# Left rows and left probabilities in idle slots of the left tile, and 576 columns of one weight granule kept in SBUF

## The chip, the cores and the metric

One core of one Trainium2 chip runs the kernel. The metric is the device time of one execution in microseconds; lower is better. In the profile the engines are PE (matrix products), PEld (its weight loads), DVE (VectorE), ACT (ScalarE), POOL (GpSimd) and SP (SyncE); 16 transfer engines move data between HBM and SBUF.

## The reference

```python
xn = layernorm(x)                         # x: 2048 rows of 1024
mem = mem0                                # 8 rows
for s in range(64):                       # segments of 32 rows, in order
    h = concat(mem, xn[32*s : 32*s+32])   # 40 rows
    q, k, v = h @ Wq, h @ Wk, h @ Wv      # 32 heads of 128
    p = softmax(mask(q @ k.T * 128**-0.5))
    o = (p @ v) @ Wo
    mem = o[:8]; out[32*s : 32*s+32] = o[8:]
result = x + out + B(xn)                  # B: two rows picked by a router go through a gated MLP, the others pass
```

Every segment needs the memory rows that the segment before has made, so the 64 segments run one after the other, and each uses all four weight matrices: 32 MB in bf16, more than SBUF holds.

## The kernel before, in words

The weights are cut into 64 granules of 128 partitions x 2048 columns (512 KB). Granules 0 to 47 are the six phases of a segment (query, key, query, key, value, value halves, eight granules each), granules 48 to 63 the sixteen steps w of the output projection. 44 granules are resident in SBUF (tiles `wres`). The other twenty are streamed in every segment through five slots (pool `wstream`, tile `g`): `fetch` (L329) issues the load on SP's queue from a packed copy in DRAM (`wsc`), and `after` calls it as soon as the granule that held a slot has been used. Granule 11 is kept whole in PSUM (`KEPT`), so its slot is filled by four copies and no load; of granule 25, columns 1024 to 2047 are kept in PSUM and copied into the slot (L349), columns 0 to 1023 are loaded: 256 KB, from a `wsc` copy of that width.

The order of the work is written out by hand: every engine carries out its instructions in the order in which the program emits them. `hook(p, kc, fn)` puts `fn` behind granule kc of phase p; `todo` is a list of such entries for the next segment; inside the projection the code names w.

A segment's main pass treats 24 of its 32 rows and the 8 memory rows (`ST`, L645). The remaining 8 rows of four segments in a row, s = 4G to 4G + 3, form one "left" tile of 32 rows that goes through the weights once for the four (`STL`, `left_pass` at L628): its queries are made in segment j = 1, its keys in j = 2, its values in j = 0 of its own group (j = s mod 4). Queries and keys go by DRAM (`ql_d`, `LX`) to each segment. The attention of each segment treats main and left rows together: `scores`, `exponent`, `soften` (L552 to L563) and `attend` (products L578 and L580, copies L585 and L587). The left outputs of segment j are written to slot j of `OTL` (128 x 4 x 8 x 32), and in j = 3 `project(WL, ...)` (L700) multiplies the four slots by the output weights, the last five steps of it as `todo` in the next segment.

Tiles that the change touches:

- `PL` (128 x 256): the probabilities that belong to the left keys, eight columns per block for segment j, zeros elsewhere. POOL clears the columns of the segment before at (1, 0) (L591), `soften` writes them (L560) and transposes the tile (L563).
- `XL` (128 x 256): the left rows of x, loaded by four DMAs on POOL's queue (L289), once in j = 0 for the next group's normalization (`norm_left`, L294) and once in j = 3 for the sum (`sum_left`, L303; added to `WL` by an identity product, L738, at w = 1).
- the scratch for the left queries, slots 2 and 3 of `OTL`: ACT copies PSl there and issues the store to `ql_d` (L669, L672).
- `OTL` itself, made at its first use in a group.

Of the kernel before, what the change touches and what calls it, by code (L numbers as in the profile page):

```python
# [20 lines left out]
KEPT_PART = 25  # L21
LEFT_OUT = 35
NEG = -30000.0

# [4 lines left out]
def kernel(  # L29
# [17 lines left out]
    P = 128  # L47
# [46 lines left out]
    const = ctx.enter_context(tc.tile_pool(name="const", bufs=1))  # L94
    dram = ctx.enter_context(tc.tile_pool(name="dram", bufs=1, space=DRAM))
    wstream = ctx.enter_context(tc.tile_pool(name="wstream", bufs=N_SLOT))
    one = ctx.enter_context(tc.tile_pool(name="one", bufs=1, reuse_waits="tile"))
    psA = ctx.enter_context(tc.tile_pool(name="psA", bufs=2, space=PSUM))
    psL = ctx.enter_context(tc.tile_pool(name="psL", bufs=1, space=PSUM))
# [8 lines left out]
    def columns(g, s):  # L108
        if s > 0 and g == KEPT_WHOLE:
            return None  # L110
        return slice(0, 1024 if s > 0 and g == KEPT_PART else 2048)

# [13 lines left out]


    IDENT = const.tile([P, P], BF16, name="IDENT")
    make_identity(nc, IDENT[:, :])

    XS = const.tile([P, 256], BF16, name="XS")
    XN = const.tile([P, 256], BF16, name="XN")
    PL = const.tile([P, 4, 2, 32], BF16, name="PL")
    CT = const.tile([P, 32], F32, name="CT")
# [14 lines left out]
    nc.vector.memset(XN[:, :], 0.0)  # L149
    nc.gpsimd.memset(PL[:, :, :, :], 0.0)  # L150
    nc.vector.memset(NMSK, 0.0)
# [123 lines left out]
    def new_st(s):  # L275
        PTx = turn(XN)
        st = one.tile([P, KC, SEG], BF16, tag="st", name="ST")
        nc.scalar.copy(out=gview(st)[:, :, :, 0:XM], in_=PTx[:, :, :, 0:XM])
        return st
# [4 lines left out]

    def load_left(G):
        t = one.tile([P, 256], BF16, tag="xl", name="XL")
        o4 = x2[4 * G * SEG:4 * (G + 1) * SEG, :].rearrange("(s r) d -> s r d", s=4)
        for g in range(4):
            nc.gpsimd.dma_start(out=t[32 * g:32 * (g + 1), :], in_=o4[:, XM:SEG, 256 * g:256 * (g + 1)])  # L289
        return t  # L290
# [40 lines left out]

    def part(t, jq):
        return t[:, 512 * jq:512 * (jq + 1)]


    def keep(g, t):
        for c, K in KEPT_COLS[g].items():
            turned = PTB.rearrange("p (i r) -> p i r", i=4)
            for i in range(4):
                nc.tensor.transpose(out=turned[:, i, :], in_=t[:, 512 * c + P * i:512 * c + P * (i + 1)],  # L340
                                    identity=IDENT[:, :])
            XK = one.tile([P, 512], BF16, tag="vl", name="XK")
# [47 lines left out]
    load_seg(0)  # L390
    XL0 = load_left(0)
    OB = one.tile([P, 256], BF16, tag="bA", name="MEM0")
# [102 lines left out]
    for s in range(NSEG):  # L495
# [53 lines left out]
        def soften(half):  # L549
            S8 = SPS.rearrange("p i a k -> p (i a) k")  # L550
            DN = one.tile([P, 8], F32, tag="nm", name="DN")
            nc.vector.tensor_reduce(out=DN[:, :], in_=S8, axis=AX.X, op=ALU.add)  # L552
            nc.vector.reciprocal(out=DN[:, :], in_=DN[:, :])
            PT2 = one.tile([P, 2, 4, 64], BF16, tag=("bA", "bE")[half], name="PT2")
            PTm, PTl = PT2[:, 0], PT2[:, 1]
            PM = PTl.rearrange("p i q -> p (i q)").rearrange("p (b k) -> p b k", b=8)
            PLt = PL.rearrange("p i a k -> p (i a) k")
            dnb = DN[:, :].unsqueeze(2)
            nc.vector.tensor_tensor(out=PM, in0=S8[:, :, 0:32], in1=dnb.to_broadcast([P, 8, 32]), op=ALU.mult)
            nc.vector.tensor_tensor(out=PLt[:, :, XL * j:XL * (j + 1)], in0=S8[:, :, 32:NK],  # L560
                                    in1=dnb.to_broadcast([P, 8, XL]), op=ALU.mult)
            nc.vector.transpose(out=PTm.rearrange("p i q -> p (i q)"), in_=PM.rearrange("p b k -> p (b k)"))
            nc.vector.transpose(out=PTl.rearrange("p i q -> p (i q)"), in_=PLt.rearrange("p b k -> p (b k)"))  # L563
            PTs[half] = (PTm, PTl)

        def attend(half, ph):
# [15 lines left out]
            for jl in range(2):  # L582
# [4 lines left out]
                copy(out=left_out()[:, j, :, h0:h0 + 4].rearrange("p r i -> p i r"), in_=ov[:, :, SEG:NK])  # L587

        def clear_pl():
            jp = (j + 3) % 4  # L590
            nc.gpsimd.memset(PL.rearrange("p i a k -> p (i a) k")[:, :, XL * jp:XL * (jp + 1)], 0.0)  # L591

        def get_left():
            nxt["xl"] = load_left(G if j == 3 else G + 1)

        def prep_left():
            if j == 0:
                norm_left(nxt["xl"], G + 1)
            else:
                sum_left(nxt["xl"], G)  # L600

        for at, fn in todo:
            hook(*at, fn)
        todo = []
        hook(1, 0, clear_pl)
        if s > 0:
# [8 lines left out]
        if s + 1 < NSEG:  # L615
            hook(2, 0, lambda: load_seg(s + 1))
        if j == 3 or (j == 0 and G + 1 < NT):
            hook(2 if j else 3, 0, get_left)
            hook(5, 3, prep_left)
# [5 lines left out]

        def left_pass(PSl, g, Gv, first_, last_):
            for jq in range(4):
                nc.tensor.matmul(PSl[32 * jq:32 * jq + 32, :], lhsT=STL[:, g % KC, :], rhs=part(Gv, jq),  # L628
                                 start=first_, stop=last_, tile_position=(0, 32 * jq))

        left_before = False
        for p, (mat, half) in enumerate(PHASES):
# [8 lines left out]
            for kc in range(KC):  # L641
                g = 8 * p + kc
                Gv = granule(g)
                for jq in range(4):
                    nc.tensor.matmul(PSm[32 * jq:32 * jq + 32, :], lhsT=ST[:, kc, :], rhs=part(Gv, jq),  # L645
                                     start=(kc == 0), stop=(kc == KC - 1), tile_position=(0, 32 * jq))
# [12 lines left out]
            if mat < 2:  # L659
# [35 lines left out]

        def project(PS, w, Gv, lhs, last):
            for hs in range(2):
                h = 2 * w + hs
                for g in range(4):
                    nc.tensor.matmul(PS[32 * g:32 * g + 32, 0:256], lhsT=lhs(h),  # L700
                                     rhs=Gv[:, D * hs + 256 * g:D * hs + 256 * (g + 1)], start=False,
                                     stop=(last and hs == 1), tile_position=(0, 32 * g), skip_group_check=True)
# [12 lines left out]
        late = home_w[len(carried):]  # L715
        final = (carried or late or [None])[-1]
        behind = []
        for w in range(16):
# [8 lines left out]
            if j == 3:  # L727
                if w in home_w:
                    fn = lambda w=w, Gv=Gv: project(WL, w, Gv, lhs_left, w == final)
                    if w in late:  # L730
# [5 lines left out]
                if w == 1:  # L736
                    WL = psL.tile([P, 512], F32, tag="accl", name="WL")
                    nc.tensor.matmul(WL[:, 0:256], lhsT=IDENT[:, :], rhs=nxt["xl"][:, :], start=True, stop=False,  # L738
                                     skip_group_check=True)
                if w >= 1:  # L740
                    for w_, Gv_ in behind:
                        project(WL, w_, Gv_, lhs_left, False)
# [26 lines left out]
        for fn in fill[n1:]:  # L769
            fn()  # L770
        if j == 3:
            def store_left(G=G, WL=WL):
                OL = one.tile([P, 256], BF16, tag="vl", name="OL")
                nc.scalar.copy(out=OL[:, :], in_=WL[:, 0:256])
                o4 = out2[4 * G * SEG:4 * (G + 1) * SEG, :].rearrange("(s r) d -> s r d", s=4)
                for g in range(4):
                    nc.gpsimd.dma_start(out=o4[:, XM:SEG, 256 * g:256 * (g + 1)], in_=OL[32 * g:32 * (g + 1), :])
            todo.append(((2, 4), store_left))
        if s + 1 < NSEG:
# [118 lines left out]
```

## Time and profile before

| | |
|---|---|
| median of 3 runs | 1993.74 us (1986.56 to 2001.2) |
| the profiled execution's own time | 1984.53 us |
| its span, first to last instruction | 1982.9 us, mean granted clock 0.957 |
| PE busy | 1630.3 us (82%) |
| DVE, ACT, POOL busy | 883.9, 733.5, 436.4 us |
| moved by DMA | 712.42 MB, mean 359 GB/s |

The span is one profiled execution; the three runs scatter around a time some 9 us longer. The program has three parts: the first segment with the loading of the resident weights, 63 segments of about 28 us, and the gated MLP at the end. Groups of instructions are named by line, engine, and written tile<-read tiles; behind the bar stand busy time, mean of one, and the idle time of the engine before them with what ended it. A row of the timeline has start, duration, engine, line and operation.

### The profile page before, as it was taken

The numbers are of one execution on the slowest core, as the hardware profiler recorded it, in microseconds if no ns is written. First come the engines' busy times: TensorE is split into PE (matmuls) and PEld (weight loads), VectorE is DVE, ScalarE is ACT, GpSimd is POOL, SyncE is SP. The second block draws the span as 40 slices with busy tenths as digits, with TensorE's granted clock in tenths as the row PEclk, the third lists the DMA queues.
The fourth block names the chain that finished last, engine by engine and source line by source line (L and its number), as shares of the span: only waits on it lengthen the run. The fifth ranks groups of instructions, "written<-read, shape, count | busy, mean of one in ns | idle before, by whom it ended". The sixth has DMA issues, their size and how long they took to land. (4 is left out here: it accounts for less than half of the span.)

```text
span 1982.9 us, 82788 instructions
## 1 busy us (share of the span) xinstructions
PE 1630.3 (82%) x36080; PEld 893.2 (45%) x36080; DVE 883.9 (45%) x2848; ACT 733.5 (37%) x1995; POOL 436.4 (22%) x883
## 2 busy tenths in 40 slices
PE   3468898989888888989888888989888898988863
PEld 1224444444454444445454444545444444544443
DVE  5834444444444434444454444444444444444430
ACT  1124343434334343433444344443434343343330
POOL 3112213112221311222121221222131122212110
PEclk8669999999999999999999999999999999999995
DMA  9999999999999999999999999999999999999998
GB/s 370 403 340 371 353 358 347 366 362 348 375 336 367 366 336 357 360 367 346 372 356 364 356 360 372 350 371 364 361 355 350 355 362 362 333 369 354 353 391 333
DMA packets 232123, 712.42 MB, mean 359 GB/s; under 512 B 39296, under 2 KB 53168, under 8 KB 231760
## 3 DMA queue, kind: packets, MB, share of 16 engines
q1 hardware_dynamic: 194384, 671.18, 90.9%
q0 software_dynamic: 28736, 28.09, 4.4%
q10 hardware_dynamic: 8640, 7.87, 1.2%
q8 instruction: 282, 4.62, 0.9%
q14 instruction: 81, 0.66, 0.1%
HBM read 694.32 MB, written 22.29 MB: 361 GB/s over the span
## 5 line engine op out<-in xcount | busy, mean ns | idle before, releaser
L645 PE MATMUL PSm<-wres,ST 128*32 128x512 bf16 x8448 | 719.3, 386 | 10.7 <-DVE ST L283 5.4
L645 PEld LDWEIGHTS <-ST 128*32 128x32 bf16 x12288 | 327.0, 96 | 439.2 <-issue 219.6
L645 PE MATMUL PSm<-g,ST 128*32 128x512 bf16 x3840 | 392.4, 388 | 125.6 <-DMA g<-wsc 116.0
L700 PE MATMUL WO<-wres,OT 128*32 128x256 bf16 x5632 | 234.2, 280 | 21.4 <-DMA wres<-in_A_Wo_dram 11.4
L700 PEld LDWEIGHTS <-OT 128*32 128x32 bf16 x8192 | 203.9, 98 | 105.5 <-issue 82.3
L661 ACT CAST XB<-PSm 128x512 bf16<-128x512 f32 x256 | 150.5, 588 | 264.1 <-PE PSm L645 264.0
L453 POOL DMA_DIRECT2D LX<-ql_d x63 | 33.6, 534 | 954.4 <-DVE OTL L587 371.7
L628 PE MATMUL PSl<-wres,STL 128*32 128x512 bf16 x2112 | 201.4, 390 | 5.6 <-ACT VL L688 3.7
L349 DVE COPY g<-KEPT 128x512 bf16<-128x512 bf16 x252 | 95.1, 419 | 195.4 <-PE PSm L645 146.1
L763 POOL DMA_DIRECT2D out_dram<-XN x256 | 129.4, 513 | 226.7 <-DVE XN L761 220.9
L253 POOL DMA_DIRECT2D XN<-in_A_x_dram x256 | 128.8, 508 | 205.1 <-PE PSm L645 69.1
L520 DVE COPY KT<-BT 128x512 bf16<-128x512 bf16 x128 | 53.4, 417 | 245.8 <-PE BT L510 203.3
L700 PE MATMUL WO<-g,OT 128*32 128x256 bf16 x2560 | 133.0, 282 | 34.2 <-DMA g<-wsc 23.2
L684 ACT CAST VM<-PSm 128x512 bf16<-128x512 f32 x128 | 79.5, 621 | 107.3 <-PE PSm L645 107.3
L510 PE MATMUL BT<-IDENT,XB 128*128 128x128 bf16 x1024 | 102.3, 223 | 15.9 <-ACT XB L661 14.5
L510 PEld LDWEIGHTS <-XB 128*128 128x128 bf16 x1024 | 58.7, 98 | 121.9 <-ACT XB L661 71.2
L628 PEld LDWEIGHTS <-STL 128*32 128x32 bf16 x3072 | 83.8, 98 | 65.8 <-issue 15.9
L537 DVE TENSOR_TENSOR BS<-BS,CT 128x96 f32<-128x96 f32 (+1 forms) x256 | 59.7, 233 | 106.8 <-PE BS L530 102.3
L515 ACT COPY QT<-BT 128x512 bf16<-128x512 bf16 x128 | 75.2, 588 | 84.0 <-PE BT L510 43.8
L761 DVE CAST XN<-WO 128x128 bf16<-128x128 f32 x64 | 18.7, 292 | 196.0 <-ACT XN L760 196.0
L578 PEld LDWEIGHTS <-VM 32*128 32x128 bf16 x2048 | 69.7, 91 | 75.7 <-issue 71.5
L547 ACT ACTIVATE BS<-BS 128x320 f32<-128x320 f32 x128 | 54.1, 423 | 119.6 <-DVE BS L543 119.5
(161 smaller groups left out, 2413.8 us busy)
## 6 DMA issues: line engine op xcount, KB each, us to landing
g<-wsc SPq DMA_DIRECT2D x1134, 512.0 KB, 6.0
g<-wsc SPq DMA_DIRECT2D x63, 256.0 KB, 5.0
LX<-ql_d POOLq DMA_DIRECT2D x63, 128.0 KB, 6.1
MW<-in_B_w_gate_dram SPq DMA_DIRECT2D x16, 448.0 KB, 9.5
MW<-in_B_w_up_dram SPq DMA_DIRECT2D x16, 448.0 KB, 9.0
wres<-in_A_Wq_dram SPq DMA_DIRECT2D x12, 512.0 KB, 11.5
MW<-in_B_w_down_dram SPq DMA_DIRECT2D x12, 512.0 KB, 10.1
wres<-in_A_Wk_dram SPq DMA_DIRECT2D x11, 512.0 KB, 13.1
```

Of the source, the lines that this page charges most:

```text
L253: nc.gpsimd.dma_start(out=XN[32 * g:32 * g + XM, :], in_=x2[s * SEG:s * SEG + XM, 256 * g:256 * (g + 1)])
L349: copy(out=t[:, 512 * c:512 * (c + 1)], in_=KEPT_COLS[g][c])
L510: nc.tensor.transpose(out=PTq[:, il, :, :].rearrange("p j r -> p (j r)"), in_=XB[:, il * P:(il + 1) * P], identity=IDENT[:, :])
L515: nc.scalar.copy(out=QT[half][:, :, :], in_=pv)
L537: nc.vector.tensor_tensor(out=S4, in0=S4, in1=m, op=ALU.add)
L578: nc.tensor.matmul(o, lhsT=VM[half][q0:q0 + 32, il * P:(il + 1) * P], rhs=PTm[q0:q0 + 32, il, 0:NK], start=True, stop=False, tile_position ...
L628: nc.tensor.matmul(PSl[32 * jq:32 * jq + 32, :], lhsT=STL[:, g % KC, :], rhs=part(Gv, jq), start=first_, stop=last_, tile_position=(0, 32 ...
L645: nc.tensor.matmul(PSm[32 * jq:32 * jq + 32, :], lhsT=ST[:, kc, :], rhs=part(Gv, jq), start=(kc == 0), stop=(kc == KC - 1), tile_position= ...
L661: nc.scalar.copy(out=XB[:, :], in_=PSm[:, :])
L684: nc.scalar.copy(out=VM[half][:, :], in_=PSm[:, :])
L700: nc.tensor.matmul(PS[32 * g:32 * g + 32, 0:256], lhsT=lhs(h), rhs=Gv[:, D * hs + 256 * g:D * hs + 256 * (g + 1)], start=False, stop=(last ...
L763: nc.gpsimd.dma_start(out=out2[s * SEG:s * SEG + XM, 256 * g:256 * (g + 1)], in_=OB[32 * g:32 * g + XM, :])
```

## The change

`PL` and the tile `XL` are given up. The left probabilities live in slot 3 of `OTL`, which is otherwise written only in j = 3; slot 3 is zeroed once per group at (2, 3) of j = 0, and by columns at (1, 0) of j = 1 to 3. The left rows for the normalization are loaded into slot 1 of `OTL`; the scratch for the left queries moves to slots 1 and 2. The rows for the sum are loaded at w = 9 of j = 3 into a tile with the tag `vl` (the place of the left values); `sum_left` runs at (1, 6) of the next segment and the identity product at (2, 2), as the last product of `WL` rather than the first. In the place freed, behind the slots and the other tiles, lies `HB`: columns 0 to 575 of granule 25, copied from its slot in the first segment. From then on only columns 576 to 1023 are loaded, and the matmuls read from `HB` what lies there: the first quarter whole, the second in two pieces of 64 and 448 columns. `ST` gets a pool of its own ahead of the slots, so the slots keep their addresses.

```diff
+HB_COLS = 576
...
+    front = ctx.enter_context(tc.tile_pool(name="front", bufs=1, reuse_waits="tile"))
     wstream = ctx.enter_context(tc.tile_pool(name="wstream", bufs=N_SLOT))
     one = ctx.enter_context(tc.tile_pool(name="one", bufs=1, reuse_waits="tile"))
+    rest = ctx.enter_context(tc.tile_pool(name="rest", bufs=1))
...
-        return slice(0, 1024 if s > 0 and g == KEPT_PART else 2048)
+        return slice(HB_COLS, 1024) if s > 0 and g == KEPT_PART else slice(0, 2048)
...
+    HB = rest.tile([P, HB_COLS], BF16, name="HB")
-    PL = const.tile([P, 4, 2, 32], BF16, name="PL")
-    nc.gpsimd.memset(PL[:, :, :, :], 0.0)
...
-        st = one.tile([P, KC, SEG], BF16, tag="st", name="ST")
+        st = front.tile([P, KC, SEG], BF16, tag="st", name="ST")
...
-    def part(t, jq):
-        return t[:, 512 * jq:512 * (jq + 1)]
+    def pieces(s, g, t, jq):
+        c0, c1 = 512 * jq, 512 * (jq + 1)
+        if s == 0 or g != KEPT_PART or c0 >= HB_COLS:
+            return [(0, 512, t[:, c0:c1])]
+        n = min(c1, HB_COLS) - c0
+        return [(0, n, HB[:, c0:c0 + n])] + ([(n, 512, t[:, c0 + n:c1])] if n < 512 else [])
 
     def keep(g, t):
+        if g == KEPT_PART:
+            nc.vector.tensor_copy(out=HB[:, :], in_=t[:, 0:HB_COLS])
...
-            PLt = PL.rearrange("p i a k -> p (i a) k")
+            PLt = zeros_and_left().rearrange("p r h -> p (r h)").rearrange("p (b k) -> p b k", b=8)
...
+        def zeros_and_left():
+            return left_out()[:, 3]
+
         def clear_pl():
-            jp = (j + 3) % 4
-            nc.gpsimd.memset(PL.rearrange("p i a k -> p (i a) k")[:, :, XL * jp:XL * (jp + 1)], 0.0)
+            z = zeros_and_left().rearrange("p r h -> p (r h)")
+            if j:
+                z = z.rearrange("p (b k) -> p b k", b=8)[:, :, XL * (j - 1):XL * j]
+            nc.gpsimd.memset(z, 0.0)
 
         def get_left():
-            nxt["xl"] = load_left(G if j == 3 else G + 1)
+            nxt["xl"] = load_left(G + 1, left_out()[:, 1].rearrange("p r h -> p (r h)"))
 
         def prep_left():
-            if j == 0:
-                norm_left(nxt["xl"], G + 1)
-            else:
-                sum_left(nxt["xl"], G)
+            norm_left(nxt["xl"], G + 1)
...
-        hook(1, 0, clear_pl)
+        hook(*((1, 0) if j else (2, 3)), clear_pl)
...
-        if j == 3 or (j == 0 and G + 1 < NT):
-            hook(2 if j else 3, 0, get_left)
+        if j == 0 and G + 1 < NT:
+            hook(4 if s == 0 else 3, 0, get_left)
             hook(5, 3, prep_left)
...
-                        XBl = left_out()[:, 2:4].rearrange("p s r h -> p (s r h)")
+                        XBl = left_out()[:, 1:3].rearrange("p s r h -> p (s r h)")
...
                 if w == 1:
                     WL = psL.tile([P, 512], F32, tag="accl", name="WL")
-                    nc.tensor.matmul(WL[:, 0:256], lhsT=IDENT[:, :], rhs=nxt["xl"][:, :], start=True, stop=False,
-                                     skip_group_check=True)
...
+            if w == 9 and j == 3:
+                LR = load_left(G, one.tile([P, 256], BF16, tag="vl", name="XL")[:, :])
...
+            def add_left(WL=WL, LR=LR):
+                nc.tensor.matmul(WL[:, 0:256], lhsT=IDENT[:, :], rhs=LR, start=False, stop=True, skip_group_check=True)
...
-            todo.append(((2, 4), store_left))
+            todo.insert(0, ((1, 6), lambda G=G, LR=LR: sum_left(LR, G)))
+            todo += [((2, 2), add_left), ((2, 4), store_left)]
```

More of the change, by code (lines that the diff above doesn't have):

```diff
@@ L283, in mem_to_st, with load_left @@
         nc.vector.tensor_copy(out=gview(st)[:, :, :, XM:SEG], in_=PTm[:, :, :, XM:SEG])
-    def load_left(G):
-        t = one.tile([P, 256], BF16, tag="xl", name="XL")
+    def load_left(G, t):
         o4 = x2[4 * G * SEG:4 * (G + 1) * SEG, :].rearrange("(s r) d -> s r d", s=4)
@@ L390 @@
     load_seg(0)
-    XL0 = load_left(0)
+    XL0 = load_left(0, one.tile([P, 256], BF16, tag="vl", name="XL0")[:, :])
     OB = one.tile([P, 256], BF16, tag="bA", name="MEM0")
@@ L624, with left_pass @@
         hook(5, 6, lambda: attend(0, 1))
-        def left_pass(PSl, g, Gv, first_, last_):
+        def left_pass(PSl, g, Gv, first_, last_, s=s):
             for jq in range(4):
-                nc.tensor.matmul(PSl[32 * jq:32 * jq + 32, :], lhsT=STL[:, g % KC, :], rhs=part(Gv, jq),
-                                 start=first_, stop=last_, tile_position=(0, 32 * jq))
+                for c0, c1, rhs in pieces(s, g, Gv, jq):
+                    nc.tensor.matmul(PSl[32 * jq:32 * jq + 32, c0:c1], lhsT=STL[:, g % KC, :], rhs=rhs,
+                                     start=first_, stop=last_, tile_position=(0, 32 * jq))
         left_before = False
@@ L644 @@
                 for jq in range(4):
-                    nc.tensor.matmul(PSm[32 * jq:32 * jq + 32, :], lhsT=ST[:, kc, :], rhs=part(Gv, jq),
-                                     start=(kc == 0), stop=(kc == KC - 1), tile_position=(0, 32 * jq))
+                    for c0, c1, rhs in pieces(s, g, Gv, jq):
+                        nc.tensor.matmul(PSm[32 * jq:32 * jq + 32, c0:c1], lhsT=ST[:, kc, :], rhs=rhs,
+                                         start=(kc == 0), stop=(kc == KC - 1), tile_position=(0, 32 * jq))
                 if g in KEPT_COLS and s == 0:
@@ L694, with project @@
             norm_seg(s + 1)
-        def project(PS, w, Gv, lhs, last):
+        def project(PS, w, Gv, lhs, last, first_=False):
             for hs in range(2):
@@ L700, in project @@
                     nc.tensor.matmul(PS[32 * g:32 * g + 32, 0:256], lhsT=lhs(h),
-                                     rhs=Gv[:, D * hs + 256 * g:D * hs + 256 * (g + 1)], start=False,
+                                     rhs=Gv[:, D * hs + 256 * g:D * hs + 256 * (g + 1)], start=(first_ and hs == 0),
                                      stop=(last and hs == 1), tile_position=(0, 32 * g), skip_group_check=True)
@@ L715 @@
         late = home_w[len(carried):]
-        final = (carried or late or [None])[-1]
+        first_left = j == 3
         behind = []
@@ L728 @@
                 if w in home_w:
-                    fn = lambda w=w, Gv=Gv: project(WL, w, Gv, lhs_left, w == final)
+                    fn = lambda w=w, Gv=Gv: project(WL, w, Gv, lhs_left, False)
                     if w in late:
@@ L737 @@
                     WL = psL.tile([P, 512], F32, tag="accl", name="WL")
-                    nc.tensor.matmul(WL[:, 0:256], lhsT=IDENT[:, :], rhs=nxt["xl"][:, :], start=True, stop=False,
-                                     skip_group_check=True)
                 if w >= 1:
                     for w_, Gv_ in behind:
-                        project(WL, w_, Gv_, lhs_left, False)
+                        project(WL, w_, Gv_, lhs_left, False, first_left)
+                        first_left = False
                     behind = []
```

## The prediction

> **What bounds the kernel now.** I read the page's busy times, its DMA parts and the groups first, then the waits of the sync queue, then the window table.
>
> ```profile
> span 1982.9 us, 82788 instructions
> PE 1630.3 (82%) x36080; PEld 893.2 (45%) x36080; DVE 883.9 (45%) x2848; ACT 733.5 (37%) x1995; POOL 436.4 (22%) x883
> DMA  9999999999999999999999999999999999999998
> ...
> q1 hardware_dynamic: 194384, 671.18, 90.9%
> q0 software_dynamic: 28736, 28.09, 4.4%
> q10 hardware_dynamic: 8640, 7.87, 1.2%
> ...
> HBM read 694.32 MB, written 22.29 MB: 361 GB/s over the span
> ...
> L645 PE MATMUL PSm<-g,ST 128*32 128x512 bf16 x3840 | 392.4, 388 | 125.6 <-DMA g<-wsc 116.0
> ...
> L700 PE MATMUL WO<-g,OT 128*32 128x256 bf16 x2560 | 133.0, 282 | 34.2 <-DMA g<-wsc 23.2
> ```
>
> The transfer engines are busy in every slice, and the matrix engine's longest waits are for streamed granules: 116.0 + 23.2 = 139 us, 2.2 us in each of 63 segments. So the streamed bytes set most of the time. But not all of it:
>
> ```profile
> SPq L329 <- PE PSm L645: 465.5, 613, 4.3
> ...
> 994.00:1006.00 12.00, 9.41 (x200) 4.35 (x198) 6.81 (x19) 4.85 (x10) 3.43 (x7) 1.00 0.99 372
> 1007.50:1023.50 16.00, 14.79 (x382) 10.03 (x382) 5.15 (x22) 6.27 (x20) 3.78 (x9) 1.00 0.92 334
> 1040.00:1064.00 24.00, 21.21 (x454) 10.86 (x450) 9.77 (x30) 9.72 (x23) 4.77 (x10) 1.00 0.96 354
> 1242.00:1247.00 5.00, 4.64 (x106) 3.78 (x94) 1.63 (x6) 1.79 (x4) 2.51 (x6) 1.00 0.82 284
> ```
>
> The first line says that the next load waits for a slot that PE must free. In the windows the first engine column is PE, the last three are granted clock, DMA share and GB/s. In the middle of a segment (994 to 1006) PE is busy 9.41 of 12 us and DMA is full: DMA leads. From the first attention products of a group's last segment (j=3) into the next segment (1007.5 to 1023.5) PE is busy 14.79 of 16 us and DMA falls to 0.92, to 0.82 just behind such a border (1242 to 1247): here PE leads, and what delays PE there leaves the transfer engines idle. Both parts add up to the time.
>
> **The change part by part.** *Fewer bytes.* Granule 25 is loaded as 448 columns instead of 1024:
>
> ```profile
> g<-wsc SPq DMA_DIRECT2D x63, 256.0 KB, 5.0
> ```
>
> 63 loads go from 128 packets of 2048 B to 128 of 896 B, 147,456 B less each. The price of a packet comes from the queue rows: q1, nearly all 4096 B packets, has 0.909 x 16 x 1982.9 us for 671.18 MB, 43.0 ns per 1000 B, so 176 ns per packet; q10 holds the 1024 B packets: 0.012 x 16 x 1982.9 us for 7.87 MB, 48.4 ns per 1000 B, 49.5 ns per packet. A line through both has 41.2 ns per 1000 B, so 1152 B less is 47.4 ns, times 8 packets per engine 0.38 us per segment, 23.9 us in all. The bounds: if 896 B cost as much as 1024 B, 1024 B are saved: 42.2 ns, 21.3 us; if bytes alone count, 147,456 B at 361 GB/s, 0.41 us, 25.7 us. I take 23.9, by the line.
>
> [...]
>
> How much of the 23.9 us arrives? DMA leads where granule 25 is loaded (second segment half), and there are 2.2 us of waits per segment to take the 0.38 us from; but the window 1040 to 1064 (a j=1 segment) stands at 0.96, and a lead is of no use where PE is late. I take 0.85, an estimate between the shares 0.82 and 0.99: **-20.3 us**. Ends: 0.3 (only every third load) and 1.
>
> *The left probabilities in slot 3 of the left tile.* In j=3 the copies of the left outputs (L587) write slot 3 themselves. So ACT's first copy OTL<-WO now waits until VectorE's second softmax has transposed its probabilities (L563); before, they had separate tiles. The timeline of four of the sixteen j=3 segments, the first shown and the last among them:
>
> ```profile
> 323.08 0.45 DVE L563 STREAM_TRANSPOSE PT<-PL 128x256 bf16<-128x256 bf16 x1
> 323.28 0.31 ACT L587 CAST OTL<-WO 128x32 bf16<-128x32 f32 x1
> ...
> 1007.19 0.45 DVE L563 STREAM_TRANSPOSE PT<-PL 128x256 bf16<-128x256 bf16 x1
> 1007.22 0.31 ACT L587 CAST OTL<-WO 128x32 bf16<-128x32 f32 x1
> 1007.58 0.17 PE L578 MATMUL WO<-PT,VM 32*128 32x40 bf16 x1
> ...
> 1457.88 0.31 ACT L587 CAST OTL<-WO 128x32 bf16<-128x32 f32 x1
> 1458.55 0.45 DVE L563 STREAM_TRANSPOSE PT<-PL 128x256 bf16<-128x256 bf16 x1
> ...
> 1913.86 0.31 ACT L587 CAST OTL<-WO 128x32 bf16<-128x32 f32 x1
> 1914.47 0.45 DVE L563 STREAM_TRANSPOSE PT<-PL 128x256 bf16<-128x256 bf16 x1
> ```
>
> The transpose ends after the copy's start by 0.25, 0.42, 1.12 and 1.06 us: mean 0.71. Queued behind the copy on ACT are OT<-BT, OTL<-BT and the copy of VM; PE's next product (1007.58, 0.05 us behind the end of the OTL copy) needs the bank that the copy empties. So PE stops by about 0.71 us, at the start of the stretch in which PE leads: what is late next is the freeing of slots, and the transfer engines idle longer. 16 x 0.71 = 11.4 us at the full price, zero if the next DMA waits swallow it. PE has hardly a gap for 16 us behind it (14.79 busy), so I take 0.85 here too: **+9.7 us**.
>
> *The scratch for the left queries moves to slots 1 and 2.* In j=1 the second half's scratch is stored by a DMA that ACT issues; slot 1 is then written by L587 of that same segment, no longer slot 2 a segment later:
>
> ```profile
> ql_d<-OTL ACTq DMA_DIRECT2D x30, 128.0 KB, 5.5
> ...
> 1058.02 0.33 ACTq L672 DMA_DIRECT2D ql_d<-OTL  x1
> ...
> 1064.21 0.31 ACT L587 CAST OTL<-WO 128x32 bf16<-128x32 f32 x1
> ```
>
> Issue plus 5.5 us is 1063.5, 0.7 us ahead of the copy: mostly covered, but thin. From 0 to 15 x 0.7 = 10.5 us were landings and copies to swap places; by this row it is near zero: **+1 us**.
>
> *Left rows' x.* The load for the sum goes from the middle of j=3 to w=9, behind LX on POOL's queue, ahead of the four stores of XN; its sum goes to VectorE in the next segment, ahead of the copies for granule 25; its product from W's start to (2,2), ahead of OL.
>
> ```profile
> XL<-in_A_x_dram POOLq DMA_DIRECT2D x128, 16.0 KB, 5.6
> ...
> L289 POOL DMA_DIRECT2D XL<-in_A_x_dram x128 | 75.0, 592 | 3.5 <-DMA XN<-in_A_x_dram 3.3
> ...
> 1012.95 0.54 POOL L453 DMA_DIRECT2D LX<-ql_d  x1 [15.53 <-PE WL L700]
> 1016.15 2.04 POOL L763 DMA_DIRECT2D out_dram<-XN  x4 [2.66 <-DVE XN L761]
> 1022.45 2.02 POOL L253 DMA_DIRECT2D XN<-in_A_x_dram  x4 [4.10 <-PE BT L460]
> 1025.92 2.40 POOL L777 DMA_DIRECT2D out_dram<-OL  x4 [1.45 <-ACT OL L774]
> ...
> 1020.36 0.75 DVE L349 COPY g<-KEPT 128x512 bf16<-128x512 bf16 x2 [2.13 <-PE PSm L645]
> 1025.08 0.42 DVE L520 COPY KT<-BT 128x512 bf16<-128x512 bf16 x1 [3.96 <-PE BT L510]
> ...
> 1024.02 0.40 PE L700 MATMUL WL<-wres,OTL 128*32 128x256 bf16 x8
> ```
>
> The four issues end at 1013.49 + 4 x 0.59 = 1015.86, inside POOL's 2.66 us idle; the last lands near 1015.3 + 5.6 = 1020.9. VectorE's sum then holds the copies of 1020.36 by about 1 us, and 3.96 us of idle time follow before KT. PE needs the sum at 1024.4, 3 us later. Cost 0; without that cover, PE would stop at (2,2) in PE's own stretch, 16 x 1 us. The product itself moves within that stretch. The zeroing of slot 3 (before: 64 columns per segment; now 256 at j=0) sits between the loads ending at 1024.47 and the stores at 1025.92: 0.
>
> *The split granule.* Its second quarter is two matmuls (64 and 448 columns), one more in 63 main and 15 left passes. Four matmuls take PE some 0.2 us (x8 rows 0.61, x4 rows 0.40), so 0.05 us each, 78 x 0.05 = 3.9 us bare; it lies where PE waits for DMA: **+1 us**. The copy into HB runs once.
>
> Sum: -20.3 + 9.7 + 1 + 1 = **-8.6 us**. Against the execution's own time of 1984.53 us that is 1975.9. The three runs of before have a median of 1993.74, 9.2 us above it; scaled (-0.43%), 1985.1.
>
> **The rivals.** *A: the bytes arrive whole.* If PE catches up behind the new wait and DMA sets the time everywhere, the gain is 23.9 to 25.7 us, 1968 to 1970. For it: share 9 in every slice, 139 us of DMA waits. Against: 0.82 and 0.92 where PE leads. A byte limit would make this the time too, for the whole span's 361 GB/s; the 372 GB/s of one window speak against a fixed one. [...] Chance 0.25.
>
> *B: slower.* PE's stretch decides. The OTL<-WO wait in j=3 costs its full 11.4 us, the j=1 wait 1.8, the split matmuls 3.9: 17.1 us; where PE leads, only 0.3 of the lead arrives, 7.2 us. Together +9.9 us: 2003.6. It decides once less than 17.1 / 23.9 = 0.72 of the saving arrives. For it: 0.92 at the very place of the wait. Against: DMA waits in every segment. Chance 0.2.
>
> *C: the bytes saved are hidden anyway and the waits too:* no change, 1993.7; for it speaks that the five slots are refilled as PE frees them (465.5 us); against, that DMA is full in the middle of each segment. Chance 0.1. My forecast has 0.45.
>
> **How the numbers follow.** A measurement of this kernel can tell about 1%, 20 us, from no change (its three runs span 14.6 us). A mostly ends above 1% faster (0.8 of 0.25), the forecast in 0.1 of its cases: 0.25. B ends over 1% slower in half its cases, and runs that scatter add 0.03: 0.13. Within 1%: 0.62. The range: A's end 1968 below, B's price to about 2003 above; the forecast alone would have 1976 to 1995.
>
> **What would show it.** Right: the granule 25 load in the issue list at 112 KB, q1's MB down by 9.3, the wait OTL<-WO behind DVE L563's successor near 0.7 us in j=3, segments j=1 and j=2 shorter by some 0.3 us, the borders j=3 to j=0 not. Wrong: PE's waits for g<-wsc don't fall, or PE waits at (2,2) for the sum, or the j=3 wait isn't there and the time falls by 24 us.

## The result and the profile after

The changed kernel takes 2002.99 us (median of 20 runs, 1989.9 to 2011.79), the kernel before beside it on the same chip 1990.18 us (20 runs, 1976.73 to 2001.2): ratio 1.0063, 95% interval 1.0041 to 1.0084, so 12.5 us slower (8 to 17). The profiled execution took 2007.49 us at a mean granted clock of 0.939 (before 0.957). In what follows, microseconds come from (ratio - 1) x 1990 us, and the intervals of differences between two runs from the intervals of both.

The profile page of the changed kernel; the DMA row is the busy share by slices, the q rows are packets, MB and share:

```profile
span 2005.8 us, 83006 instructions
PE 1649.3 (82%) x36158; PEld 898.6 (45%) x36158; DVE 881.8 (44%) x2849; ACT 734.7 (37%) x1995; POOL 439.3 (22%) x882
DMA  9999999899999999999999999999999999999998
...
q1 hardware_dynamic: 194384, 661.89, 89.6%
q0 software_dynamic: 28704, 27.95, 4.4%
q10 hardware_dynamic: 8640, 7.87, 1.1%
...
HBM read 684.88 MB, written 22.14 MB: 352 GB/s over the span
...
L658 PE MATMUL PSm<-g,ST 128*32 128x512 bf16 (+1 forms) x3777 | 392.3, 391 | 110.3 <-DMA g<-wsc 96.4
...
L713 PE MATMUL WO<-g,OT 128*32 128x256 bf16 x2560 | 136.3, 290 | 32.4 <-DMA g<-wsc 24.2
...
g<-wsc SPq DMA_DIRECT2D x63, 112.0 KB, 4.4
```

The bytes are gone as planned: 9.29 MB less on q1 (671.18 to 661.89), 112 KB per load. PE's waits for streamed granules fell too, 139.2 to 120.6 us. But q1's packets kept the transfer engines for 0.896 x 2005.8 = 1797 us, before for 0.909 x 1982.9 = 1802 us: 5 us less, not the 23.9 us at which the bytes were priced. The rate over the span fell from 361 to 352 GB/s.

The waits of the two kernels, first before, then after (engine, written tile, line, <- whom it waited for: sum in us, count, longest):

```profile
PE WO L578 <- ACT OTL L587: 2.2, 5, 0.7
```

```profile
PE WO L586 <- ACT OTL L595: 21.1, 25, 1.7
ACT OTL L595 <- DVE PT L571: 15.3, 14, 1.6
...
ACT OTL L595 <- DMA ql_d<-OTL: 0.8, 2, 0.4
```

ACT's copy into slot 3 (L595) now waits for VectorE's transpose (L571), as forecast, and PE behind it: PE's wait for that copy grew by 18.9 us. In the timeline of one j=3 segment after (start, duration, engine, line, and in brackets the engine's idle time with what ended it):

```profile
1015.21 0.27 ACT L593 CAST OT<-WO 128x128 bf16<-128x128 f32 x1 [0.80 <-PE BT L588]
...
1016.15 0.45 DVE L571 STREAM_TRANSPOSE PT<-OTL 128x256 bf16<-128x256 bf16 x1
1016.69 0.30 ACT L595 CAST OTL<-WO 128x32 bf16<-128x32 f32 x1 [1.21 <-DVE PT L571]
...
1017.03 0.19 PE L586 MATMUL WO<-PT,VM 32*128 32x40 bf16 x1 [1.30 <-ACT OTL L595]
```

PE stands still for 1.30 us and goes on 0.04 us behind the end of the copy of 1016.69. The window that holds this standstill and the work behind it, against the row 1007.5 to 1023.5 of before, 16 us and one segment each (PE, PEld, DVE, ACT, POOL, clock, DMA share, GB/s):

```profile
1015.40:1031.40 16.00, 14.62 (x341) 9.76 (x333) 4.97 (x22) 5.06 (x18) 4.95 (x9) 0.79 0.90 303
```

Clock 0.79 instead of 1.00, 303 GB/s instead of 334. Over the 63 segments, before and after:

```profile
130.10:1922.00 1791.90, 1553.94 (x34701) 849.63 (x34705) 801.73 (x2636) 711.56 (x1945) 401.17 (x805) 0.99 0.97 358
```

```profile
130.80:1946.60 1815.80, 1571.60 (x34778) 854.70 (x34782) 798.43 (x2631) 712.77 (x1946) 403.97 (x805) 0.97 0.96 348
```

By the place in a group (means over the segments from the ninth to the last but two, worked out from the copies that end each segment), j=0 takes 29.60 us (before 28.79), j=1 28.63 (28.57), j=2 28.07 (28.12), j=3 29.14 (28.29). The loss lies in j=3, where ACT waits, and in the j=0 behind it; j=1 and j=2 gained nothing.

### The profile page after: what moved, and what is told of

The parts are those of the page before. It is cut to its first block, busy times and chain, and to the rows that moved or that the text cites. A ratio compares the mean times of both kernels' runs of the same rounds, so it can differ in the third digit from the quotient of the medians.

```text
span 2005.8 us, 83006 instructions
## 1 busy us (share of the span) xinstructions
PE 1649.3 (82%) x36158; PEld 898.6 (45%) x36158; DVE 881.8 (44%) x2849; ACT 734.7 (37%) x1995; POOL 439.3 (22%) x882
## 3 DMA queue, kind: packets, MB, share of 16 engines
q1 hardware_dynamic: 194384, 661.89, 89.6%
## 5 line engine op out<-in xcount | busy, mean ns | idle before, releaser
L658 PE MATMUL PSm<-g,ST 128*32 128x512 bf16 (+1 forms) x3777 | 392.3, 391 | 110.3 <-DMA g<-wsc 96.4
L713 PE MATMUL WO<-wres,OT 128*32 128x256 bf16 x5632 | 245.1, 290 | 17.2 <-DMA wres<-in_A_Wo_dram 10.5
L713 PEld LDWEIGHTS <-OT 128*32 128x32 bf16 x8192 | 209.6, 101 | 103.2 <-issue 76.1
L461 POOL DMA_DIRECT2D LX<-ql_d x63 | 33.6, 533 | 1004.9 <-DVE OTL L595 714.0
```

Source lines behind the costliest of these rows:

```text
L658: nc.tensor.matmul(PSm[32 * jq:32 * jq + 32, c0:c1], lhsT=ST[:, kc, :], rhs=rhs, start=(kc == 0), stop=(kc == KC - 1), tile_position=(0, 3 ...
```

## The experiments

The theory at the outset: the wait on slot 3 costs more than forecast, and the saved bytes bring less. The rivals: that the moved sum, or the halved clock, or the matmuls' pieces take the time, or that the bytes do arrive. The letters in the expectations name the theory that each number belongs to.

**1. A tile of its own for the left probabilities** (e1, against the changed kernel):

```diff
+    PL = rest.tile([P, 256], BF16, name="PL")
...
-            PLt = zeros_and_left().rearrange("p r h -> p (r h)").rearrange("p (b k) -> p b k", b=8)
+            PLt = PL.rearrange("p (b k) -> p b k", b=8)
```

> The change, but the left probabilities keep a tile of their own (zeroed as before), so that the left-output copies of j=3 wait for no transpose; the 576 columns are read from a resident granule's columns instead of HB (the values of those columns are another granule's). Theory W (the wait in j=3 costs the time: 1.1 us of stopped PE in each of 16 segments, and more halved clock behind it): the time falls by 15 to 30 us below the change, to a ratio of 0.990 to 0.998 against before. Theory S (the late rows for the sum cost the time in j=0): it stays at the change's 1.006. Theory H (the saved bytes don't arrive, and many small costs add up): falls by at most 10 us, 1.001 to 1.006.

Measured: 1979.3 us, ratio 0.996 (0.9928 to 0.9992). PE's wait for ACT's copy is down to 4.7 us:

```profile
PE WO L586 <- ACT OTL L595: 4.7, 11, 0.7
```

From 1.0063 to 0.996 are 20 us (13 to 28), inside theory W's 15 to 30: the role of slot 3 alone costs more than the whole change loses.

**2. The bytes alone** (e2, against the kernel before: granule 25's load of 448 columns and the split matmuls, nothing moved):

```diff
-        return slice(0, 1024 if s > 0 and g == KEPT_PART else 2048)
+        return slice(HB_COLS, 1024) if s > 0 and g == KEPT_PART else slice(0, 2048)
```

> Before, with nothing moved: only the 448-column load and the split matmuls, the 576 columns read from a resident granule's columns (other values). It measures the gain alone. By the prediction's term 20 to 24 us less than before, ratio 0.988 to 0.990. Theory W expects the same (0.988 to 0.992). Theory H: the lead is lost wherever PE leads, ratio 0.996 to 1.000.

Measured: 1984.24 us, 0.9976 (0.994 to 1.0013): 5 us at most likely, 12 at the most. Its page:

```profile
span 1987.8 us, 82929 instructions
...
q1 hardware_dynamic: 194384, 661.89, 90.4%
...
L653 PE MATMUL PSm<-g,ST 128*32 128x512 bf16 (+1 forms) x3777 | 393.4, 391 | 112.0 <-DMA g<-wsc 102.5
```

0.904 x 1987.8 = 1797 us of q1, as in the changed kernel: without the wait on slot 3, the engines' packets still take only 5 us less. So the lost gain isn't that wait's doing. (This execution ran 5 us above the run's median.) The packets say where it went: in the trace of before the 151,296 packets of 4096 B on q1 took a mean of 174.2 ns, in e2 the same number took 176.5. Over 16 engines these 2.3 ns are 22 us (17 against the 174.7 ns of a second trace of before, e16), most of the 23.9 us priced.

**3. The moves alone** (e3, the changed kernel without `HB`, granule 25 loaded as before):

```diff
-HB_COLS = 576
+HB_COLS = 0
```

> The change without HB: columns 0 to 1023 of granule 25 are loaded as before, everything else as changed. It measures the costs alone. Theories W and S: before plus 25 to 35 us, ratio 1.012 to 1.018. Theory H: 1.006 to 1.010.

Measured: 2009.77 us, 1.011 (1.0059 to 1.0161): 22 us slower (12 to 32), which doesn't part the theories. Bytes and moves add up within their intervals (0.9976 x 1.011 = 1.0086, the change 1.0063).

**4. The sum's rows as before** (e4, the changed kernel with its own tile for them, loaded and added at the old places):

```diff
+            if j == 3:
+                nxt["xl"] = load_left(G, XLR[:, :])
...
+                    nc.tensor.matmul(WL[:, 0:256], lhsT=IDENT[:, :], rhs=nxt["xl"], start=True, stop=False,
```

> The change, but the rows for the sum are loaded at (2, 0) of j=3 into a tile of their own, summed at (5, 3) and added at w = 1 as before; the 576 columns are read from a resident granule's columns (other values). Theory S: back to 0.990 to 0.996 of before. Theory W: stays within 5 us of the change, 1.003 to 1.008. Theory H: falls by up to 8 us, 1.002 to 1.006.

Measured: 1995.02 us, 1.0049 (1.0021 to 1.0077), 0.14% below the change, inside both intervals: the late sum costs nothing that these runs can tell.

**5. Fewer columns, real places** (e8, the changed kernel with 320 columns in `HB` and the own tile of e1):

```diff
-HB_COLS = 576
+HB_COLS = 320
+    PL = rest.tile([P, 256], BF16, name="PL")
```

> The change, with a tile of its own for the left probabilities, and with HB cut to 320 columns to make room for it; all values as in the reference. Theory W: no wait in j=3, 320/576 of the bytes' gain: ratio 0.995 to 0.999. If the slot's role isn't the cause, 1.003 to 1.008.

Measured: 1984.0 us, 0.9988 (0.9961 to 1.0014): no change that can be told, as theory W had it. Without slot 3's double use the edit is harmless, and the bytes saved by 320 columns bring nothing visible.

**6. Left probabilities first** (e9, the changed kernel; in the second half of j=3 VectorE writes and transposes the left probabilities before the main ones):

```diff
+            if j == 3 and half == 1:
+                PTm, PTl = PTl, PTm
...
+            if j == 3 and half == 1:
+                nc.vector.tensor_tensor(out=PM, in0=S8[:, :, 0:32], in1=dnb.to_broadcast([P, 8, 32]), op=ALU.mult)
+                nc.vector.transpose(out=PTm.rearrange("p i q -> p (i q)"), in_=PM.rearrange("p b k -> p (b k)"))
```

> The change, with one order on VectorE turned round: in j=3 the second half's left probabilities are written and transposed first, then the main ones (transposed in place), so that slot 3 is free 0.85 us earlier. Theory W: the wait in front of OTL<-WO falls from 1.1 us to about 0.25, the time by 0.75 to 0.85 of what a tile of its own gave (20 us): 15 to 17 us below the change, ratio to before 0.996 to 1.001. If the wait wasn't the cause, 1.004 to 1.009.

Measured: 1988.29 us, 1.0013 (0.9989 to 1.0037): 10 us back (4 to 16; 15 to 17 were expected), with ACT's wait down from 15.3 to 5.0 us in all:

```profile
ACT OTL L602 <- DVE PT L575: 5.0, 10, 1.0
```

10.3 us less of waiting for 10 us of time: the standstill is paid about in full.

**7. The first products later** (e6, the changed kernel; in j=3 the attention's two product groups go from (5, 4) and (5, 6) to (5, 7) and w = 2):

```diff
+        hook(5, 7 if j == 3 else 4, lambda: attend(0, 0))
+        if j < 3:
+            hook(5, 6, lambda: attend(0, 1))
```

> The change, with the first half's attention products of j=3 moved back: from (5, 4) and (5, 6) to (5, 7) and to w = 2 of the projection, so that VectorE's transposes are done when the copies come, and PE has other work meanwhile. All values as in the reference. Theory W (either form): as the kernel with a tile of its own, ratio 0.993 to 1.000. If the later products themselves are late for the projection: the copies ahead of w = 0 hold PE instead, and the ratio stays above 1.002.

Measured: 2003.11 us, 1.0098 (1.0071 to 1.0126). In this order the second group's products go to PE behind the projection's first steps, and the result is off by a relative 0.43; which sums are wrong, and why, the run doesn't show. The instructions are those of the change, in another order. ACT's wait for the transpose fell to 1.3 us in all and the j=3 segment still took 30.18 us, since now the copies hold PE ahead of the projection, as the second expectation had it:

```profile
PE WO L714 <- ACT OTL L595: 16.9, 16, 1.1
```

It doesn't speak for or against the wait's price.

**8. The clock.** In the changed kernel's profile the clock is halved for 116.0 us of the 63 segments, before for 44.4 us (a second trace of before, e16: 37.5). Two kernels fill the standstill with 16 products whose values nobody reads. The first (e5) put them into idle columns of a bank that ACT was about to copy:

```diff
+        def keep_busy():
+            for _ in range(16):
+                nc.tensor.matmul(nxt["wo"][:, 416:512], lhsT=IDENT[:, :], rhs=res_tiles[24][:, 0:96], start=True, stop=True,
```

> The change, with 16 products of 128x128x96 whose result nobody reads, placed on PE between the two halves of the first attention products of j=3, where PE now stands still for 1.1 us. The wait stays, the clock is kept. [...] Theory W2 (the stopped 1.1 us alone, the clock only goes along): clock may return, time stays within 3 us of the change or rises, 1.005 to 1.009.

Measured: 2004.29 us, 1.0081 (1.005 to 1.0112). Its timeline shows why it tells nothing: the filler itself waited for the copy and ran behind the standstill, 0.84 us more on the path.

```profile
1023.62 0.84 PE L600 MATMUL WO<-wres,IDENT 128*128 128x96 bf16 x16 [1.54 <-ACT OTL L595]
```

The second (e10) has a bank of its own:

```diff
+            DUMMY = psL.tile([P, 512], F32, tag="accl", name="DUMMY")
...
+                nc.tensor.matmul(DUMMY[:, 0:96], lhsT=IDENT[:, :], rhs=res_tiles[24][:, 0:96], start=True, stop=True,
```

> The change, with the same 16 products as in the earlier run, but written to the idle bank of the left sums, so that they don't wait for ACT and fall into the standstill of j=3. Theory W1 (part of the cost is the halved clock): granted clock back to 0.948 or more, the time 5 to 12 us below the change, ratio 1.000 to 1.004. Theory W2 (the standstill alone): within 3 us of the change, 1.005 to 1.009, whatever the clock.

Measured: 1995.17 us, 1.0053 (1.0027 to 1.008). The wait stands, the clock is back (mean over the runs 0.9528; the change 0.9432, before 0.953), halved for 47.8 us only:

```profile
ACT OTL L595 <- DVE PT L571: 17.6, 16, 1.6
```

The time fell by 0.1% (2 us; by the intervals from 9 us less to 5 us more) against the change, as theory W2 had it. So the standstill costs, and the halved clock that comes with it costs, by these intervals, less than half of the 20 us.

**9. The same cut in four granules** (e7, e2 with granules 13, 29 and 41 cut as well):

```diff
+LESS = (13, 29, 41)
...
+        if s > 0 and g in LESS:
+            return slice(HB_COLS, 2048)
```

> The run on bytes alone, with the same cut of 576 columns in three more granules (13, 29 and 41): four times the bytes left out, 37 MB (the columns are read from a resident granule, other values). If a fixed share of the saved transfer time arrives: the one cut gave 0 to 12 us (middle 5), so four give 20, ratio 0.990; the prediction's 0.85 would give 80 us, 0.960. Theory H (PE leads nearly everywhere else): 0.992 to 0.998, with the DMA share falling to about 0.94. Theory D (the one cut was too small to be seen among runs that scatter by 8 us): 0.960 to 0.975.

Measured: 1946.8 us, 0.9813 (0.9777 to 0.9849): 37 us (30 to 44) for four times 23.9, a share of 0.39. That lies between the theories: none of the expected ranges holds it.

```profile
span 1942.0 us, 83397 instructions
...
q1 hardware_dynamic: 194384, 634.02, 89.4%
...
L656 PE MATMUL PSm<-g,ST 128*32 128x512 bf16 (+1 forms) x3588 | 387.5, 385 | 71.4 <-DMA g<-wsc 61.2
```

q1's packets took 0.894 x 1942.0 = 1736 us, 66 less than before and not 96, since each took longer (0.894 x 16 x 1942.0 us / 634.02 MB = 43.8 ns per 1000 B; before 43.0). And of the 66 only 37 left the time (41 in the two profiles): the rest is time in which q1 had no packet under way. So part of a saved byte's price is lost in longer packets and part in idle time.

**10. Less work for PE** (e11: before, without the left projection of the resident steps, 88 products per group; e12: the same with the four cuts):

```diff
-                    if w in late:
-                        fill.append(fn)
-                    else:
+                    if w not in late:
+                        pass
+                    if 0:
```

> Before, without the left projection's products of the eleven resident steps w (their sums are left out): 88 products less, some 2.4 us of PE, in each of 16 groups, all in the stretch from j=3's projection to phase 2 of j=0. Theory P (PE leads there, at the full price): up to 38 us less, ratio 0.981 to 0.988. If transfers set the time there: less than 8 us, 0.996 to 1.000.

> The same products left out of the kernel with four cut granules (other values in the cut columns). Against the run without the products: theory P says that the stretch where PE leads swallowed the rest of the bytes' gain, so four cuts now bring more than the 37 us that they brought with the products, 50 to 70 us, ratio to before 0.945 to 0.960. If the rest was lost in the transfer engines themselves (longer packets), again about 37 us: 0.962 to 0.970.

Measured: e11 1974.27 us, 0.9963 (0.9936 to 0.9991); e12 1935.2 us, 0.9768 (0.9734 to 0.9802). PE's busy time fell by 28 us (1630.3 to 1601.9), the time by 7, and the four cuts bring 39 us (30 to 48) on top, as without. For the stretch from j=3 to j=0, "PE leads, so the bytes don't count" falls: with PE relieved there, they count no more than they did. PE's work elsewhere wasn't varied.

**11. A sixth slot** (e13, before with N_SLOT = 6; granule 26 shares granule 24's resident tile to make the place, the bytes are those of before):

```diff
-N_SLOT = 5
+N_SLOT = 6
+SHARED = 26
...
+        if g == SHARED:
+            res_tiles[g] = res_tiles[24]
+            return
```

> Before, with six slots instead of five: granule 26 is neither loaded nor kept, its products read granule 24's tile instead (other values), and the place goes to the sixth slot; streamed bytes per segment as before. Theory Q (transfers run short of queued loads: in the traces a 4 KB packet takes 183 ns with one load outstanding, 177 with two, 173 with three or more, and the DMA share falls from 0.99 to 0.93): 5 to 20 us less than before, ratio 0.990 to 0.9975. Theory D (the engines are at their rate whatever stands in the queue): 0.998 to 1.002.

Measured: 1916.08 us, 0.9642 (0.961 to 0.9674): 71 us less, more than three times the upper end of what theory Q allowed.

```profile
span 1914.3 us, 82985 instructions
...
q1 hardware_dynamic: 194240, 670.65, 92.1%
...
HBM read 693.79 MB, written 22.29 MB: 374 GB/s over the span
...
L649 PE MATMUL PSm<-g,ST 128*32 128x512 bf16 x3840 | 391.6, 386 | 47.1 <-DMA g<-wsc 41.4
...
L704 PE MATMUL WO<-g,OT 128*32 128x256 bf16 x2560 | 134.3, 282 | 16.4 <-DMA g<-wsc 7.9
```

The load queue's waits for the landing of the load that went into the same slot before, with five slots and with six:

```profile
SPq L329 <- DMA g<-wsc: 380.3, 536, 3.0
```

```profile
SPq L333 <- DMA g<-wsc: 154.3, 260, 2.1
```

One more load may be under way, and with the same bytes PE's waits fall from 139 to 49 us, the packets from 43.0 to 42.1 ns per 1000 B, and the rate rises from 361 to 374 GB/s. (The one resident load that is left out, 512 KB in the first segment, is some 1.4 us of this by the same 43.0 ns.) On the mean 2.8 loads were under way before and 3.2 here, counting those whose landing the trace has. So before, the engines were not at a fixed rate: with five slots, how many loads may be under way held the kernel back more than the bytes did.

**12. The cuts with six slots** (e14 one, e15 four; the diffs of e2 and e7 on e13):

> The run with six slots, with the one cut of 576 columns of granule 25 (other values there too). Against six slots alone: theory Q 14 to 22 us less (0.6 to 0.9 of 23.9 us), theory D 5 to 12 us as with five slots.

> The run with six slots, with four cut granules (13, 25, 29, 41; other values). Against six slots alone: theory Q 57 to 85 us less (0.6 to 0.9 of 95.6 us), ratio to before 0.950 to 0.967; theory D 30 to 45 us, 0.975 to 0.984 where six slots alone bring nothing.

Measured: 1911.29 us, 0.9625 (0.9589 to 0.9661), and 1894.59 us, 0.9531 (0.9494 to 0.9569): 3 us (6 more to 13 less) and 22 us (12 to 32) below e13. Theory Q missed: the share of the price (0.14 and 0.23) didn't grow with the sixth slot. Theory D's 5 to 12 and 30 to 45 us lie at the edge of the intervals. With only 49 us of waits left there is less for bytes to take; that this is the reason wasn't tested.

**13. How far the numbers scatter** (e16, the kernel before again, one execution):

> Before once more, for a second trace of it: how far the mean of a 4 KB packet (174.7 ns), the halved-clock time (44 us) and the transfer engines' busy time in 63 segments (1746 us) scatter between two executions. Theory D needs the 4 KB packet of the cut kernels (176 to 178 ns) to lie within that scatter; theory Q has it longer because fewer bytes are queued.

Measured: 1982.41 us, q1 at 91.2% of 1980.8 us, 1806 us, 4 us from the profile of before. The 66 us of e7 stands far above such a difference, the 5 us of e2 doesn't: "hardly less" is all that can be said of it. The 4096 B packets of q1 took a mean of 174.7 ns here and 174.2 in the first trace; the 176.5 to 177.3 ns of the cut kernels (e2, the change, e7) lie outside that, so theory D's condition isn't met: the packets that were left did get longer.

**14. Slots paid for with resident granules**, nothing left out (e17: a sixth slot, granule 27 streamed; e18: seven slots, granules 7 and 27 streamed):

```diff
-N_SLOT = 5
+N_SLOT = 6
+MORE = [27]
...
+    streamed = sorted(streamed + MORE)
```

> Before, with a sixth slot in the place of one resident granule (27), which is streamed instead: 43 resident, 21 streamed, all values as in the reference. The sixth slot brought 71 us; 512 KB more per segment are 128 packets of 176 ns over 16 engines, 1.41 us, 89 us in all, of which a share of 0.2 to 0.4 has shown, 18 to 36 us. Expected if the slots are the bound: 35 to 53 us less than before, ratio 0.973 to 0.982. If the bytes count in full after all: 15 to 20 us more, 1.008 to 1.010.

> The same with two granules (7 and 27) given for two slots: 42 resident, 22 streamed, seven slots; all values as in the reference. With six slots the waits for loads were down to 49 us, so a seventh can bring at most that, while 89 us of transfers come on top at a growing share: between the six-slot exchange and 30 us above it, ratio 0.975 to 0.997.

Measured: e17 1976.55 us, 0.9933 (0.9909 to 0.9958); e18 2024.95 us, 1.0178 (1.0144 to 1.0213). The page of e17, then of e18:

```profile
q1 hardware_dynamic: 203456, 704.21, 92.8%
...
HBM read 727.87 MB, written 22.81 MB: 380 GB/s over the span
...
L647 PE MATMUL PSm<-g,ST 128*32 128x512 bf16 x4096 | 419.5, 389 | 104.3 <-DMA g<-wsc 96.6
```

```profile
q1 hardware_dynamic: 212528, 737.25, 93.6%
...
L647 PE MATMUL PSm<-g,ST 128*32 128x512 bf16 x4352 | 450.6, 390 | 122.8 <-DMA g<-wsc 116.4
```

Six slots move 33 MB more than before and are 13 us faster (5 to 18): e17 beats the kernels before and after the change. The expectations missed: of e17 neither the 35 to 53 us less nor the 15 to 20 us more came, and e18 was to be faster than before. Against e13 the added 33.6 MB cost 58 us (50 to 66) of some 90 at 43.0 ns per 1000 B, a share of 0.64; the next 33 MB and a seventh slot cost 49 us more. In these runs bytes added cost more of their price than bytes removed give back. For e18 there is a rival: the profile names the stores of the left queries and keys as what ended 176 us of the load queue's waits, in e13 8 us, before none. Whether they held it up wasn't tested.

```profile
SPq L331 <- DMA ql_d<-OTL: 96.0, 29, 5.6
SPq L331 <- DMA ql_d<-XBl: 80.2, 30, 3.9
```

## Why the prediction was right or wrong

It said 8.6 us faster; the kernel is 12.5 us slower. The time lies at the upper end of the stated range, the direction is that of rival B. Two steps failed, and both towards slower: the saved bytes brought 5 us instead of 20.3, and the wait cost some 20 us instead of 9.7. By its steps:

- **Fewer bytes, -20.3: failed.** The step is "DMA leads where granule 25 is loaded ... I take 0.85". The bytes alone brought 5 us (e2, 0.2 of the price; -3 to 12), 0.39 of it in e7. The price per packet was near: the 896 B packets took a median of 41 ns (after; the tenth and the ninetieth percentile of the 8064 are 41 too), 1024 B 46, 2048 B 84, so 43 ns less where 47.4 were priced. The reading "DMA is full, so DMA leads" was not: the digit 9 and the share 0.99 count an engine as busy while it holds a packet (the times of q1's packets before add up to 1802 us an engine, its 90.9%), and q1's packets took 41.0 (e18) to 43.8 ns (e7) per 1000 B. A share of busy time didn't tell here how much of a saving arrives. In e2 the packets left over took back most of what the shorter ones saved (174.2 to 176.5 ns). The row that pointed elsewhere stood in the prediction: "SPq L329 <- PE PSm L645: 465.5", the load queue waits for a slot. All such waits of this line for PE add up to 992 us, those for the landing of the slot's last load to 380 us. Sixty-three loads cut by 56% each still hold a slot each, and a sixth slot at the same bytes brought 71 us (e13). Rival A fails with the same step, and the 372 GB/s that it weighed were a hint: whole spans ran at 380 (e17) and 389 (e18). Why the packets left over get longer isn't settled; that PE's work in the stretch from j=3 to j=0 is to blame is excluded (e11, e12).
- **The wait on slot 3, +9.7: right place and mechanism, mis-sized.** 0.71 us was forecast, 0.96 us measured (the row's 15.3 us over the sixteen j=3 segments). The four segments that the 0.71 came from were a fair sample: over all sixteen, the trace of before gives 0.69. But the first products came 0.37 us earlier in the segment than before (18.47 against 18.84 us), so the copy asked earlier, while 0.71 had been read from a schedule without the wait. The factor 0.85 was wrong as well: ACT waited 15.3 us in all, PE 18.9 us longer than before, and e1 gives 20 us of time. "What is late next is the freeing of slots, and the transfer engines idle longer" fits the window with 303 GB/s; it wasn't tested by itself.
- **Scratch in slots 1 and 2, +1: right.** The wait for the store is 0.8 us in two places.
- **Left rows' x, 0: right.** VectorE waited 50.9 us for the late rows, 16 times, and PE 0.7 us once for the sum:

```profile
DVE XL L305 <- DMA XL<-in_A_x_dram: 50.9, 16, 4.2
...
PE WL L787 <- DVE XL L305: 0.7, 1, 0.7
```

  The 50.9 us lies in VectorE's slack, as e4 says: in fifteen of the sixteen groups the sum was done 2.2 to 5.2 us ahead of PE's product (forecast: 3).
- **Split matmuls, +1: not separable** from e2's 5 us.
- **The rival B** set its point right: slower once less than 0.72 of the saving arrives. 0.2 to 0.4 did. Its saving of 7.2 us is near the 5 (e2) and 8 us (e1) measured. That its costs of 17.1 us are near the measured 20 is in part luck: it put 11.4 of them on the wait, which took the 20 alone (e1). Of the signs for the forecast, the load of 112 KB, the 9.3 MB and the wait in j=3 came; that j=1 and j=2 would shorten by 0.3 us did not, though PE's waits for granules fell.

## What to carry to other kernels

Ahead of pricing bytes, look at what the load queue waits for: where it waited for a slot, a smaller load gave back 0.14 to 0.39 of its price here, and room for one more slot gave more (71 us for a slot of 2048 columns, 37 us for four cuts of 576). What the slot takes the place of counts too: paid for with a resident granule, 13 of the 71 us were left (e17). The tile lent to VectorE's data added 15.3 us of waits in ACT's queue here. The length of such a wait is to be read from the schedule that the change will make; at this place, where PE was busy 14.79 of 16 us before, 18.9 us more of PE's waiting cost 20 us (e1). The DMA row, nines in 39 of 40 slices, was the same in the kernel before and in e13, which is 71 us faster with the same bytes per segment: the row didn't tell whether the bytes set the time.

## What the runs showed of the hardware

- In the 63 segments the clock fell to a half for stretches of 3.41 us, sometimes two in a row: 116.0 us of them after, 44.4 before. The 27 falls after came behind 3.41 us in which PE was busy for 0.35 to 0.73 of the time, median 0.50; ahead of stretches that kept the whole clock the median was 0.93. That restoring the clock was worth only 2 us of 2000 (e10; 9 less to 5 more) I had not expected.
- Packets were longer where fewer loads were under way: in the trace of before, 4096 B packets took a mean of 183.6 ns with one granule load outstanding, 175.3 with two, 173.4 with three, 172.7 with four, at an unchanged median of 159 ns (counted over the 882 of 1197 loads whose landing the trace has; other ways of counting shift the figures). The mean over all of q1's was 174.2 ns with five slots, 170.8 with six (e13), 166.0 with seven (e18). That the one makes the other isn't shown.
- One core moved 380 (e17) and 389 GB/s (e18) over a whole span where it had stood at 361.
- Products into columns that ACT doesn't read still waited for ACT's copy from the same bank (e5: 1.54 us); whether the chip or the order set in the program makes them wait, the run doesn't show.
